# Form stage spread over modes 55 to 61, channel sums moved around mode 62's product, more filler matmuls, and longer store runs

## The chip, the cores and the metric

The kernel runs on one core of a Trainium2 chip. A core has TensorE (PE; its weight loads are shown as PEld), VectorE (DVE), ScalarE (ACT), GpSimd (POOL) and SyncE (SP), a memory of 128 partitions next to the engines (SBUF), an accumulator memory of 8 banks that the matmuls write (PSUM), and 16 DMA engines that move data between SBUF and the main memory. The metric is the time on the device in microseconds, the median of several runs.

## The reference

```python
q_p, k_p = phi(q), phi(k)                 # phi(x) = elu(x) + 1; 8 batches, 8 heads, 576 rows, 64 columns
kv  = einsum('bhsd,bhse->bhde', k_p, v)
z   = sum(k_p, axis=2)
x   = einsum('bhsd,bhde->bhse', q_p, kv) / (einsum('bhsd,bhd->bhs', q_p, z)[..., None] + 1e-6)
x   = x in the shape (8, 576, 512)        # heads side by side
X   = rfft(x, axis=1)[:, :64]             # 64 modes
Y   = einsum('bmd,mde->bme', X, w_r + 1j * w_i)    # one complex 512 x 512 matrix for each mode
u   = x + irfft(Y, n=576, axis=1)
out = u + maximum(u @ w_ch, 0)
```

The two weight tensors w_r and w_i hold 64 matrices of 512x512 in float32 each, 134 MB in all.

## The kernel before

**Attention.** For each batch the kernel loads q, k and v, forms the features, the 64x65 sums over k and v, the attention rows and their Fourier transform (a matmul with a constant matrix). The transformed rows of all batches end up in the tile xt_c.

**Mode pairs.** Then the 64 modes are worked through in 32 pairs (`mode_pair(p)` for modes 2p and 2p+1, `last_pair()` for modes 62 and 63, p = 31). A pair's weights are 2 MB in bfloat16, converted on the way by DMAs that POOL issues (`w_load`, L119; `w_load_last`, L131, cuts the last pair into seven DMAs). From pair 5 on there are two weight buffers: the loads of pair p+2 wait on POOL's queue until the products of pair p (L442) have been done. The products go to a PSUM tile for each mode. VectorE and ScalarE copy them out (`evacuate`, L452, L454), and eight small matmuls (`picks`, L460) bring each mode's rows into a collecting tile, which is copied on after every eighth mode. Inside a pair the order on TensorE is: products, the "mid" slot of other work, picks, the "end" slot, then `keep_warm(FILL[p])`. `keep_warm(n)` issues n matmuls of 128x512 whose result nobody uses (L425, tile zl); they are called fillers below. `pin` keeps the instructions of an engine in the order of the program.

**Other work.** The lists `work` and `slots` spread the work on x between the pairs. `share` hands a list of items out to slots in proportion to weights.
- Pairs 5 to 14: the attention rows again, in the order of the output (36 tiles of 128 rows).
- Pairs 15 to 26, the fold: the inverse transform of modes 0 to 31 is added to x, and x @ w_ch of that is formed and kept as E0 (L653 to L684).
- Pairs 27 to 29, the form stage: for each batch b, `form_z(b)` (eight matmuls, L698, copied out by ScalarE at L703) and `form_y(b)` (eight transposes, L711, copied out by VectorE at L712) make the rows of modes 32 to 55 for the end. After those of batch 0 and of batch 1 come four `fold_lead` items each (L720 to L728). That makes 24 items: "z0, y0, four folds, z1, y1, four folds, z2, y2 ... z7, y7".
- Pair 30: the channel sums of the first two tile pairs. `channels(n)` (L774, two matmuls) brings E0 into an accumulator of two banks, and `first_rows(n)` (L874, two matmuls) adds batch 0's rows of modes 32 to 55. The four PSUM banks of the form stage are given up for these accumulators ahead of pair 30.

**Last pair.** Mode 62's product goes the usual way, with four fillers before its picks and six after them. Mode 63's product (y_last, L504, 32 matmuls with 16 columns) is computed transposed, right after the fillers. Its weights' second half comes in four pieces of 256, 128, 64 and 64 KB.

**Tail.** The rows of modes 56 to 63 are formed (L914 to L925) and sent within SBUF to the other batches' rows (two DMAs, L929). Then the 18 tile pairs follow in turn: `channels(n)`, `rectified(n)` (inverse transform, L735, and Relu, L784) and `finish(n)` (inverse transform, addition to x on VectorE, L816, and the store, L790, on SP's queue). A store of one tile has runs of 2 KB in the output, one of two tiles 4 KB, one of four tiles (the batches in `QUADS`) 8 KB. The last tile pair is added and stored one tile at a time (L811).

Of the kernel before, what the change touches and what calls it, by code (L numbers as in the profile page):

```python
# [14 lines left out]
ALU = mybir.AluOpType  # L15
# [28 lines left out]
def kernel(  # L44
# [10 lines left out]
    nc = tc.nc  # L55
# [12 lines left out]
    NE = NM - NL  # L68
    NF = NM // 2
# [42 lines left out]
    LAST = NM // 2 - 1  # L112
# [309 lines left out]
    def keep_warm(n: int):  # L422

        for _ in range(n):
            pin(nc.tensor.matmul(last_ps[0], id16, wch16[:, 0, :]))  # L425
# [4 lines left out]
    def work_slot(p: int, name: str):  # L430
        for _ in range(slots.get((p, name), 0)):
            if work:
                work.pop(0)()

    def product(P, kk: int, w, dc: int):
        last = kk // 2 == LAST
        n_dc = NDL if last else NDW
        c = dc % NDC * 32
        n = 32 if dc < NDC else 2 * B
        rows = slice(0, 128) if last else HALVES[kk % 2]  # L440
        pin(
            nc.tensor.matmul(  # L442
                P[c : c + n, :], xt_cols(dc, kk, n), w[rows, dc, :],
                start=(dc < NDC), stop=(dc >= n_dc - NDC), tile_position=(rows.start, c),
                skip_group_check=True,
            )
        )

    def evacuate(kk: int, P):
        st = ystage.tile([128, D], F16, tag="ystage", bufs=2, name=f"ys{kk}")  # L450
        if kk % 2 == 0:
            pin(nc.vector.tensor_copy(out=st, in_=P))  # L452
        else:
            pin(nc.scalar.copy(out=st, in_=P))  # L454
        return st
# [9 lines left out]
    def mode_pair(p: int):  # L465
        nonlocal yt_ps
        w = w_get(p)
        kks = (2 * p, 2 * p + 1)
        if p % 4 == 0:
            yt_ps = psW.tile([128, NDC, 8, 2 * B], F32, tag="yt", bufs=1, name=f"yt{p // 4}")  # L470
        Ps = [psW.tile([128, D], F32, tag="P", bufs=2, name=f"P{kk}") for kk in kks]
        for dc in range(NDW):
            for P, kk in zip(Ps, kks):
                product(P, kk, w, dc)
        sts = [evacuate(kk, P) for P, kk in zip(Ps, kks)]
        work_slot(p, "mid")
        for kk, st in zip(kks, sts):
            picks(kk, st)
        if p % 4 == 3:
            if kks[1] < NF:  # L480
                pin(nc.vector.tensor_copy(out=YE_T[:, :, kks[1] - 7 : kks[1] + 1, :], in_=yt_ps))
            else:
                g = (kks[1] - NF) // NL + 1
                pin(nc.vector.tensor_copy(out=YL[:, :, :, g, :], in_=mode_rows(yt_ps)))
        work_slot(p, "end")
        keep_warm(FILL.get(p, 0))

    def last_pair():
        w = w_get(LAST)
        kk = NM - 2  # L490
        P = psW.tile([128, D], F32, tag="P", bufs=2, name=f"P{kk}")
        for dc in range(NDL):
            product(P, kk, w, dc)
        st = evacuate(kk, P)
        keep_warm(4)
        picks(kk, st)
        pin(nc.vector.tensor_copy(out=Y8[:, :, 0 : NL - 1, :], in_=yt_ps[:, :, 0 : NL - 1, :]))
        keep_warm(6)
        kk = NM - 1
        y_last = psW.tile([128, NDC, 2 * B], F32, tag="P", bufs=2, name="y_last")  # L500
        for dc in range(NDL):
            for ec in range(NDC):
                pin(
                    nc.tensor.matmul(  # L504
                        y_last[:, ec, :], w[:, NDL + dc, ec * 128 : ec * 128 + 128],
                        xt_cols(dc, kk, 2 * B),
                        start=(dc == 0 and ec == 0), stop=(dc == NDL - 1), skip_group_check=True,
                    )
                )
        nc.vector.tensor_copy(out=Y8[:, :, NL - 1, :], in_=y_last)  # L510
# [9 lines left out]
    PSUM = bass.MemoryType.PSUM  # L520
    psW = tc.alloc_tile_pool(name="psW", bufs=1, space=PSUM, side="left")
    psB = tc.alloc_tile_pool(name="psB", bufs=1, space=PSUM, side="right")


    n_early = n_keep + n_pre
    FILL = {**{p: 1 for p in range(20, 27)}, 27: 1, 28: 1, 29: 2, 30: 3}
    ystage = ctx.enter_context(tc.tile_pool(name="ystage", bufs=1, side="right"))
    inv_sb = ystage.tile([2 * NM, S], F16, name="inv_sb")
    inv2_sb = ystage.tile([128, S], F16, name="inv2_sb")
# [8 lines left out]
    def mode_rows(ps):  # L538
        return ps.rearrange("p c m (t b) -> p c (m t) b", b=B)
# [19 lines left out]
    def x_of(t: int):  # L559
        if t < B * NJJ:  # L560
            return x_main[t // NJJ][:, t % NJJ, :]
        i = t - B * NJJ
        return x_tail[i // 2][:, i % 2, :]
# [185 lines left out]
    pairs = []  # L749
# [5 lines left out]
    N_PRE = 2  # L755
# [3 lines left out]
    def on_bank(n: int, banks: set, ins):  # L759
        pin(ins)  # L760
        for other, theirs in users.setdefault(n, []):
            if not banks & theirs:
                tc.declare_no_dep(ins.ins, other.ins, reason="the other bank of the pair")
        users[n].append((ins, banks))
    accs: dict[int, object] = {}

    def channels(n: int):
        pool = acc_pools[n % 4 // 2]
        accs[n] = pool.tile([128, 2, D], F32, tag="acc", bufs=2, name=f"acc{n}")
        for i, t in enumerate(pairs[n]):  # L770
            for cols, src in e0_parts(t):
                on_bank(
                    n, {i},
                    nc.tensor.matmul(  # L774
                        accs[n][:, i, cols], id16, src, start=(cols.start == 0), stop=False,
                        skip_group_check=True,
                    ),
                )
# [7 lines left out]
    def store(t: int, n_t: int):  # L786
        if t < B * NJJ:
            b, jj = divmod(t, NJJ)
            r0 = b * S + BASE[b % 2]
            nc.sync.dma_start(  # L790
                out=out_rows[r0 : r0 + 512, :].rearrange("(r j) d -> r j d", j=NJJ)[:, jj : jj + n_t, :],
                in_=x_main[b][:, jj : jj + n_t, :],
            )
            return
        i = t - B * NJJ
        nc.sync.dma_start(
            out=out_rows.rearrange("(i r) d -> r i d", i=B // 2)[512:640, i : i + 2, :],
            in_=x_tail[i // 2],
        )

    QUADS = (6,)

    def finish(n: int):
        acc = accs[n]
        single = n == len(pairs) - 1
        t0 = pairs[n][0]
        add_inverse(n, 0)
        for i, t in enumerate(pairs[n]):
            if single:
                x = x_of(t)  # L810
                on_bank(n, {i}, nc.vector.tensor_tensor(out=x, in0=acc[:, i], in1=x, op=ALU.add))  # L811
                store(t, 1)
        if single:
            return
        x = x_main[t0 // NJJ][:, t0 % NJJ : t0 % NJJ + 2, :] if t0 < B * NJJ else x_tail[(t0 - B * NJJ) // 2]
        on_bank(n, {0, 1}, nc.vector.tensor_tensor(out=x, in0=acc, in1=x, op=ALU.add))  # L816
        if t0 < B * NJJ and t0 // NJJ in QUADS:
            if t0 % NJJ:
                store(t0 - 2, NJJ)
            return  # L820
        store(t0, 2)
# [24 lines left out]
        if b < N_LEAD:  # L846
            work += [lambda t=t: fold_lead(t) for t in range(b * NJJ, b * NJJ + NJJ)]
    n_form = len(work) - n_fold
    first_fold, first_form, n_form_p = NF // 2 - 1, NE // 2 - 1, 3
    fold_pairs = first_form - first_fold  # L850

    def share(n_items: int, steps: list):
# [11 lines left out]
    share(  # L864
        n_form,
        [((first_form, "end"), 6)]
        + [((p, h), 4) for p in range(first_form + 1, first_form + n_form_p) for h in ("mid", "end")],
    )

    def first_rows(n: int):  # L870
        for i, t in enumerate(pairs[n]):
            on_bank(
                n, {i},
                nc.tensor.matmul(  # L874
                    accs[n][:, i], inv2_sb[0 : 2 * NF, rows_of(t, BASE[0])], YZ[0][0 : 2 * NF, 1, :],
                    start=False, stop=False, skip_group_check=True,
                ),
            )
# [8 lines left out]
    )  # L887

    for p in range(n_early, LAST):
        if p == LAST - 1:  # L890
            assert not work
            psB.release()
            acc_pools.append(
                tc.alloc_tile_pool(name="psT0", bufs=1, space=PSUM, side="right", reuse_waits="tile")
            )
            slots[p, "mid"] = slots[p, "end"] = N_PRE
            for n in range(N_PRE):
                work += [lambda n=n: channels(n), lambda n=n: first_rows(n)]
        mode_pair(p)
    last_pair()  # L900


# [14 lines left out]
    for h in range(2):  # L917
        for ec in range(NDC):
# [3 lines left out]
                    start=(ec == 0), stop=(ec == NDC - 1),  # L922
# [5 lines left out]
    for h, eng in enumerate((nc.sync, nc.gpsimd)):  # L928
        eng.dma_start(  # L929
            out=YZ_all[64 * h : 64 * h + 64 : NF // NL].rearrange("r b z d -> r b (z d)"),  # L930
# [11 lines left out]
    def add_one(n: int, i: int):  # L942
# [8 lines left out]
            out=x_of(0), in0=accs[0][:, 0], scalar=0.0, in1=x_of(0), op0=ALU.max, op1=ALU.add  # L951
# [51 lines left out]
```

## Time and profile before

| | |
|---|---|
| median of 4 runs | 425.05 us (423.73 to 425.36) |
| the profiled execution's own time | 423.73 us |
| its span, first to last instruction | 421.9 us |
| busy: PE, DVE, ACT, POOL | 271.9, 215.3, 161.6, 56.6 us |
| mean granted TensorE clock | 0.777 |
| moved by the DMA engines | 93.19 MB, of that 81.47 MB on POOL's queue |
| weight loads, issue to landing | 12.3 us (w_r), 17.0 us (w_i) |
| products L442: idle before them for w_i | 64.3 us |

The page of the profile shows the span in 40 slices of 10.5 us: the busy share of each engine in tenths, the granted TensorE clock (PEclk) in tenths of full speed and the busy share of the DMA engines. The chain of the work that ended last is followed back from the last instruction, at each step to what released it. The view of groups gives busy time and idle time by line; the timeline gives instructions in order, with the idle time before each and what ended it; and the view of stretches gives busy times, clock and DMA share for any stretch of the span. Times in these views are microseconds from the span's start.

### The profile page before, as it was taken

To read this page: it belongs to the slowest core of one execution; us is meant where nothing else is said; L and a number is where in the kernel's file an instruction comes from. 1 tells how busy PE (TensorE), PEld (TensorE's weight loads), DVE (VectorE), ACT (ScalarE), POOL (GpSimd) and SP (SyncE) were. 2 spreads that over 40 slices of the span, in tenths; PEclk is the share of its full clock that TensorE was granted. 3 is DMA by queue.
4 is the path that set the end of the run, shared out by engine and by line. 5 is a ranking of instruction groups with operands and counts; after the bars stand their busy time and mean duration, and the time that the engine had idled before them with its cause. 6 is when DMAs were issued, how large, how long until landed. Compare 5 with 4: busy or idle time off the path is not lost.

```text
span 421.9 us, 7890 instructions
## 1 busy us (share of the span) xinstructions
PE 271.9 (64%) x3378; PEld 148.9 (35%) x3378; DVE 215.3 (51%) x447; ACT 161.6 (38%) x253; POOL 56.6 (13%) x99
## 2 busy tenths in 40 slices
PE   0348378778607644444343677968687795899992
PEld 0246267666402222222122233424243232365420
DVE  3599498886302462464544433445354243322794
ACT  4688577854301102000000243444354251231782
POOL 4222124210001111111111111101011111121000
PEclk9999886889955555555555598789899697679998
DMA  9999999999999999999999999999999999998697
GB/s 214 210 210 215 206 227 194 216 224 217 205 229 209 221 217 211 217 217 214 214 223 214 210 224 214 211 220 219 210 219 217 218 211 219 217 190 162 238 404 305
DMA packets 20802, 93.19 MB, mean 221 GB/s; under 512 B 2080, under 2 KB 11168, under 8 KB 16480
## 3 DMA queue, kind: packets, MB, share of 16 engines
q0 software_dynamic: 16512, 81.47, 94.2%
q1 hardware_dynamic: 4256, 11.22, 7.2%
q8 instruction: 26, 0.43, 0.4%
q14 instruction: 8, 0.07, 0.0%
HBM read 163.93 MB, written 9.44 MB: 411 GB/s over the span
## 4 chain that ended last, share of the span: by engine, by line
DMA 63%; PE 22%; DVE 4%; ACT 4%; issue 3%; POOL 2%; DVEq 0%; POOLq 0%; ACTq 0%
DMA w<-in_moe_w_i_dram 48%; PE P L442 8%; DMA pick_sb<-row_pick 8%; DMA k<-in_k_dram 7%; PE acc L735 3%; PE z L698 2%; PE acc L774 2%; ACT ke L213 2%; POOL w L119 1%; ACT qT L249 1%; PE zl L425 1%; DVE ys L452 1%; PE yp L711 1%; PE yt L460 1%; DVE x L299 1%
## 5 line engine op out<-in xcount | busy, mean ns | idle before, releaser
L442 PE MATMUL P<-w,xt_c 64*32 64x512 bf16 (+2 forms) x1000 | 51.3, 540 | 65.7 <-DMA w<-in_moe_w_i_dram 64.3
L452 DVE CAST ys<-P 128x512 f16<-128x512 f32 x32 | 22.1, 691 | 117.4 <-PE P L442 117.4
L454 ACT CAST ys<-P 128x512 f16<-128x512 f32 x31 | 18.1, 585 | 150.6 <-PE P L442 150.6
L119 POOL DMA_DIRECT2D w<-in_moe_w_r_dram x31 | 16.3, 526 | 245.4 <-PE P L442 114.5
L442 PEld LDWEIGHTS <-xt_c 64*32 64x32 bf16 (+2 forms) x1000 | 17.0, 127 | 83.9 <-DMA w<-in_moe_w_i_dram 47.7
L676 PE MATMUL eps<-wch,xTw 128*128 128x512 f16 x144 | 41.2, 413 | 0.0
L165 PEld LDWEIGHTS <-qT 64*128 64x128 f16 (+1 forms) x640 | 22.9, 123 | 50.5 <-issue 30.9
L165 PE MATMUL num<-kv,qT 64*128 64x65 f16 (+1 forms) x320 | 13.6, 209 | 26.1 <-ACT xt_c L350 12.6
L657 DVE TENSOR_TENSOR x_main<-ya,x_main 128x512 f32<-128x512 f32 x32 | 22.0, 689 | 14.5 <-PE ya L653 14.3
L659 ACT CAST x16w<-x_main 128x512 f16<-128x512 f32 x32 | 19.8, 618 | 23.5 <-DVE x_main L657 22.5
L165 PE MATMUL nw<-kv,qT 64*128 64x65 f16 (+1 forms) x320 | 19.0, 240 | 9.5 <-DVE x_tail L620 4.3
L684 ACT CAST E<-eps 128x512 f16<-128x512 f32 (+1 forms) x40 | 21.2, 540 | 9.7 <-PE eps L676 9.7
L460 PE MATMUL yt<-pick_sb,ys 128*128 128x16 f16 x252 | 11.7, 174 | 17.3 <-DMA pick_sb<-row_pick 10.7
L299 DVE TENSOR_TENSOR x<-num,rd 128x512 f16<-128x512 f32 x32 | 22.1, 691 | 1.1
L242 PE MATMUL qTp<-id,qe 128*128 128x128 f16 x144 | 15.9, 299 | 10.2 <-DVE qe L226 9.7
L213 ACT ACTIVATE qe<-q 128x1152 f16<-128x1152 f16 (+1 forms) x16 | 17.8, 1156 | 11.3 <-DMA q<-in_q_dram 11.3
L249 ACT COPY qT<-qTp 128x1152 f16<-128x1152 f16 x16 | 19.6, 1292 | 0.6 <-PE qTp L242 0.2
L213 ACT ACTIVATE ke<-k 128x1152 f16<-128x1152 f16 x16 | 17.7, 1152 | 4.8 <-DMA k<-in_k_dram 4.8
L460 PEld LDWEIGHTS <-ys 128*128 128x128 f16 x252 | 9.7, 102 | 27.0 <-DVE ys L452 14.9
L784 ACT ACTIVATE acc<-acc 128x512 f32<-128x512 f32 x34 | 18.1, 582 | 2.4 <-PE acc L735 1.6
L242 PEld LDWEIGHTS <-qe 128*128 128x128 f16 x144 | 13.7, 139 | 11.2 <-DVE qe L226 10.1
L119 POOL DMA_DIRECT2D w<-in_moe_w_i_dram x31 | 16.8, 543 | 4.6 <-DMA q<-in_q_dram 2.3
(114 smaller groups left out, 457.6 us busy)
## 6 DMA issues: line engine op xcount, KB each, us to landing
w<-in_moe_w_r_dram POOLq DMA_DIRECT2D x31, 1024.0 KB, 12.3
w<-in_moe_w_i_dram POOLq DMA_DIRECT2D x31, 1024.0 KB, 17.0
out_dram<-x_main SPq DMA_DIRECT2D x11, 512.0 KB, 4.0
k<-in_k_dram POOLq DMA_DIRECT2D x8, 576.0 KB, 12.7
v<-in_v_dram POOLq DMA_DIRECT2D x8, 576.0 KB, 14.8
q<-in_q_dram POOLq DMA_DIRECT2D x7, 576.0 KB, 12.7
out_dram<-x_main SPq DMA_DIRECT2D x6, 256.0 KB, 4.3
q<-in_q_dram SPq DMA_DIRECT2D x2, 576.0 KB, 4.7
```

Source lines behind the costliest of these rows:

```text
L119: nc.gpsimd.dma_start(out=w_in[p][half::2], in_=two.rearrange("g (r dc) e -> (g r) dc e", dc=NDW))
L165: mm = nc.tensor.matmul(num[hpo][orow, c0 : c0 + 65], qT[rows, hpp, h2, cols], kv_sb[rows, hpp, h2, :])
L213: pin(nc.scalar.activation(out=ev[:, c], in_=heads(nm, b, c), func=AF.Exp))
L242: nc.tensor.transpose(qT_ps[:, j], phi["q", b][:, c, j].rearrange("p o d -> p (o d)"), id16,)
L249: nc.scalar.copy(out=qT[:, :, c * NJ : (c + 1) * NJ], in_=qT_ps.rearrange("p j x -> p x j"))
L299: nc.vector.tensor_tensor(out=dst.rearrange("p (o c d) -> p o c d", o=2, c=4), in0=nv[:, :, :, 0:64], in1=rden.unsqueeze(3).broadcast_to([ ...
L442: nc.tensor.matmul(P[c : c + n, :], xt_cols(dc, kk, n), w[rows, dc, :], start=(dc < NDC), stop=(dc >= n_dc - NDC), tile_position=(rows.sta ...
L452: pin(nc.vector.tensor_copy(out=st, in_=P))
L460: nc.tensor.matmul(yt_ps[:, ec, kk % 8, :], st[:, ec * 128 : ec * 128 + 128], pick_sb)
L657: pin(nc.vector.tensor_tensor(out=x, in0=acc, in1=x, op=ALU.add))
L676: nc.tensor.matmul(e_ps, xT[:, c, :], wch16[:, c, :], start=(c == 0), stop=(c == NDC - 1))
L684: pin(nc.scalar.copy(out=dst, in_=e_ps[:, cols]))
```

## The change

It has five parts.
1. The form stage's 24 items are handed out up to the "end" slot of pair 30 (mode 61), not 29. `n_form_p` goes.
2. The form stage's PSUM banks are given up after pair 30, and the two channel sums move from pair 30 into `last_pair()`: the first ahead of mode 62's product (a new slot "start"), the second between its copy and its picks, where four fillers stood. Three fillers instead of six follow.
3. `FILL` is 5 for pairs 18 to 26 (before: none for 18 and 19, 1 for the others), 8 for 27 (1), 2 for 28 (1), 7 for 29 (2) and 7 for 30 (3).
4. `QUADS` holds batches 2, 4, 5 and 6 instead of 6 alone.
5. The last tile pair is added and stored like the others, in one piece.

```diff
     def last_pair():
         w = w_get(LAST)
         kk = NM - 2
+        work_slot(LAST, "start")
         P = psW.tile([128, D], F32, tag="P", bufs=2, name=f"P{kk}")
         for dc in range(NDL):
             product(P, kk, w, dc)
         st = evacuate(kk, P)
-        keep_warm(4)
+        work_slot(LAST, "mid")
         picks(kk, st)
         pin(nc.vector.tensor_copy(out=Y8[:, :, 0 : NL - 1, :], in_=yt_ps[:, :, 0 : NL - 1, :]))
-        keep_warm(6)
+        keep_warm(3)
...
-    FILL = {**{p: 1 for p in range(20, 27)}, 27: 1, 28: 1, 29: 2, 30: 3}
+    FILL = {**{p: 5 for p in range(18, 27)}, 27: 8, 28: 2, 29: 7, 30: 7}
...
-    QUADS = (6,)
+    QUADS = (2, 4, 5, 6)

     def finish(n: int):
         acc = accs[n]
-        single = n == len(pairs) - 1
         t0 = pairs[n][0]
         add_inverse(n, 0)
-        for i, t in enumerate(pairs[n]):
-            if single:
-                x = x_of(t)
-                on_bank(n, {i}, nc.vector.tensor_tensor(out=x, in0=acc[:, i], in1=x, op=ALU.add))
-                store(t, 1)
-        if single:
-            return
...
     share(
         n_form,
         [((first_form, "end"), 6)]
-        + [((p, h), 4) for p in range(first_form + 1, first_form + n_form_p) for h in ("mid", "end")],
+        + [((p, h), 4) for p in range(first_form + 1, LAST - 1) for h in ("mid", "end")]
+        + [((LAST - 1, "mid"), 2), ((LAST - 1, "end"), 1)],
     )
...
     for p in range(n_early, LAST):
-        if p == LAST - 1:
-            assert not work
-            psB.release()
-            acc_pools.append(
-                tc.alloc_tile_pool(name="psT0", bufs=1, space=PSUM, side="right", reuse_waits="tile")
-            )
-            slots[p, "mid"] = slots[p, "end"] = N_PRE
-            for n in range(N_PRE):
-                work += [lambda n=n: channels(n), lambda n=n: first_rows(n)]
         mode_pair(p)
+    assert not work
+    psB.release()
+    acc_pools.append(
+        tc.alloc_tile_pool(name="psT0", bufs=1, space=PSUM, side="right", reuse_waits="tile")
+    )
+    slots[LAST, "start"] = slots[LAST, "mid"] = N_PRE
+    for n in range(N_PRE):
+        work += [lambda n=n: channels(n), lambda n=n: first_rows(n)]
     last_pair()
```

More of the change, by code (lines that the diff above doesn't have):

```diff
@@ L848 @@
     n_form = len(work) - n_fold
-    first_fold, first_form, n_form_p = NF // 2 - 1, NE // 2 - 1, 3
+    first_fold, first_form = NF // 2 - 1, NE // 2 - 1
     fold_pairs = first_form - first_fold
```

## The prediction

> **What bounds the kernel now.** First the slices of the page: over the whole weight stream the DMA row stands at 9, and from slice 12 on the clock row falls to 5 and recovers only in part.
>
> ```profile
> PEclk9999886889955555555555598789899697679998
> DMA  9999999999999999999999999999999999998697
> ```
>
> So the weights (2 MB a pair, every 9.7 us) set the time up to the last pair, as long as the matmuls free each weight buffer in time. Second, the chain that ended last, to find where this stops being so. Columns: start, length, what.
>
> ```profile
> 342.41 17.39 DMA w<-in_moe_w_i_dram
> ...
> 359.85 1.95 PE P L442 x24
> 361.79 1.92 PE z L698 x8
> ...
> 371.53 0.44 PE yp L711 x7
> 371.96 1.72 PE z L698 x7
> 373.69 0.54 PE zl L425
> 374.22 1.03 PE P L442 x29
> ...
> 388.07 1.31 PE zl L425 x6
> 389.38 0.92 PE y_last L504 x32
> ```
>
> Up to 359.8 it hops from one weight load to the next; from pair 28 (modes 56, 57) on it is TensorE work without a gap: pair 29's product starts at 374.2. Its weights had been issued at 352.07 with 17.4 us to landing, so they lay there from 369.5: TensorE was 4.7 us late. Third, what this costs. The last pair's loads (L131) need pair 29's buffer, so they go out only then; and the DMA runs dry (columns: stretch, length, busy of PE, PEld, DVE, ACT, POOL, clock, DMA share, GB/s).
>
> ```profile
> 375.62 0.52 POOL L131 DMA_DIRECT2D w<-in_moe_w_r_dram  x1 [12.40 <-PE P L442]
> ```
> ```profile
> 370.00:375.00 5.00, 5.00 (x57) 2.35 (x53) 0.42 (x1) 1.41 (x3) 0.00 (x0) 0.59 1.05 223
> 375.00:376.00 1.00, 1.00 (x28) 0.81 (x14) 0.68 (x2) 0.58 (x1) 0.38 (x1) 1.00 0.47 98
> 376.00:378.00 2.00, 2.00 (x24) 1.66 (x20) 0.77 (x3) 0.59 (x1) 1.75 (x4) 1.00 0.80 156
> ```
>
> Lost: 0.53 x 1.0 + 0.20 x 2.0 = 0.9 us; since packets count where they start, I take 0.7 to 0.9. The last 64 KB piece, issued at 380.44 and 9.3 us under way, lands at 389.8; the last product y_last runs 389.2 to 390.3 because the ten fillers ahead of it end at 389.2. Fourth, the stores at the end:
>
> ```profile
> 398.00:402.00 4.00, 4.00 (x29) 1.20 (x28) 3.97 (x4) 3.39 (x7) 0.00 (x0) 1.00 0.98 389
> 406.00:412.00 6.00, 6.00 (x35) 1.54 (x35) 6.00 (x6) 5.36 (x11) 0.00 (x0) 1.00 1.03 409
> 416.00:419.00 3.00, 0.00 (x0) 0.00 (x0) 0.00 (x0) 0.00 (x0) 0.00 (x0) 0.91 1.00 382
> ```
>
> From 394 to 419 the DMA is full and the last compute ends at 415.8: the tail is the 9.4 MB of stores, and it shifts as a block with y_last.
>
> **What the skill says.** "TensorE: Matmul & The Clock Gate", Part 1 (The HAM clock gate), says the array runs at half clock after an idle window of about 3.4 us and at full clock after a busy one. The trace agrees: the stretch 278.52 to 281.93 has 0.47 us of TensorE work, the next 3.41 us are granted 0.50, and after that (busy) stretch the clock is 1.00 again. The page's section "HAM oscillation — how this bites in real kernels" describes short products between DMA waits that lose the clock each time; here 350.19 to 353.61 was busy for 1.83 of 3.42 us and the next 10 us ran at 0.50. "DMA: Bandwidth & Descriptors", "Issuing engines are not separate DMA queues", says all queues share the same 16 engines: so one late weight load can't be made up elsewhere, and stores are paid in total bytes and run lengths, as the tail windows show.
>
> **The change part by part.** The sum is against the profiled execution: span 421.9, time 423.73 (1.8 around it). The median of the four runs is 425.05, 1.3 above it; the trace doesn't show why, so I carry the difference over unchanged.
>
> *Fillers, modes 36 to 53.* Five for pairs 18 and 19, four more for 20 to 26: 38 matmuls of 128x512. Six of them took 1.31 us (chain above), 0.22 each; at half clock about 0.43 (one L676 group of four took 1.91 against 1.03). Up to 1.1 us a pair (2.2 cold), ahead of a wait: the products waited for weights 64.3 us in 22 waits. Where the wait is shorter (0.63 us before the product at 340.43) the product is late by the rest; the release of its buffer has about 4 us to spare, because pair 29's 4.7 us cost less than 1 us of DMA. So 0 on the end; without that cover 1.1 us a pair, 10 us in all. They may save re-warming in the fold stage, which is hidden too.
>
> *Form stage.* There are 24 items in this order: z0, y0, four folds of batch 0, z1, y1, four folds of batch 1, then z and y of batches 2 to 7. The old weights (6,4,4,4,4 of 22) give 6,4,5,4,5; the new ones (6,4,4,4,4,2,1 of 25) give 5,4,4,4,4,2,1. They issue no DMA. Pair 28 loses y2 and z3 (0.44 + 1.86 to the next step), gains one matmul of batch 0 (0.4) and one filler (0.2 to 0.5): 14.3 - 2.3 + 0.7 = 12.7 us with the old clock. At full clock: product 1.04, two z 1.86 (0.93 each in the chain after 375), y 0.52 and its copy 0.6, four folds about 3.0 (DVE's 0.69 add sets their pace), one matmul 0.22, picks 0.29, fillers 0.43: 8.0. Pair 27's eight fillers take 1.7 to 3.4 us after about 357.2, reach 358.9 to 360.6, and so fill most of the wait in which the clock was lost; at worst they make pair 28 0.7 late. I take the full clock from about 361 on: pair 28 ends near 368, pair 29's product starts at 369.5, and the L131 loads go out near 371, with pair 30's still running to 379.2 (362.67 + 16.5). The DMA gap of 0.7 to 0.9 goes; the last piece lands at about 389.0.
>
> *Is TensorE there by then?* Pair 29: product 1.04, y2 z3 y3 z4 2.9, picks 0.3, y4 z5 y5 z6 2.9, seven fillers 1.6: 8.7, ends 378.3, before pair 30's landing. Pair 30 from 379.25: product 1.04, y6 z7 1.4, picks 0.3, y7 0.5, fillers 1.6: 384.1. The moved channel sums of the first two tile pairs (four matmuls each: 0.53 + 0.55 in the chain) now stand on TensorE's queue, the first ahead of mode 62's product, the second behind it in place of four fillers: 1.08 to 385.2; product 0.59 (landed before, 384.06 less the gap): 385.8; second sum 1.08, picks 0.2, three fillers 0.65: 387.7. Behind them waits y_last, for weights landing to 389.0; its last four matmuls need about 0.3: end 389.3 against 390.3. So TensorE has 0.7 us to spare at the end (after the first 28 matmuls), 0.9 at pair 30 and 1.4 at pair 29. Gain 0.9 to 1.0; I take 0.9.
>
> *Stores.* 18 stores from x_main become 14, four with 8 KB runs. The one such store before ran at 416 GB/s (413 to 415), 4 KB at 409, the 2 KB runs at 383 (417 to 419): 3.1 MB gain 0.13 us, the last 512 KB at 4 KB instead of 2 KB 0.09. Against that, a first half waits for its second, 1.17 us (400.05 to 401.22 in batch 2). Up to 400 the queue holds some 0.8 us of work after the store before it (1.9 of the 2.2 MB issued are moved), so the engines may idle for up to 0.4; later the backlog covers the hold. I take 0.2: tail 0, between -0.3 and +0.4. The last add becomes one of 1.22 in place of two of 0.68 and ends at 415.8 as before; its store goes out while two others are queued.
>
> Sum: -0.9 + 0: span 421.0, time 422.8 on the profiled basis, 424.2 on the median.
>
> **The rivals.** *The gain is larger:* the unprofiled runs, 1.2 to 1.6 slower, lose more clock in modes 56 to 61, and that goes as well: 424.2 - 1.3 = 422.9. For it: the free phase of the 3.4 us window; against: the profiled run already had pair 28 mostly at half clock, so 1.5 us is about all that is left. *No gain:* the fillers don't hold the clock. Then pair 28 takes 12.7 us from 359.85 or 360.4 to at most 373.1, L131 goes out 0.5 to 1 us earlier, and the added work eats that: pair 29 8.7 (8.0 before) to 381.8, from pair 30's start to y_last 8.45 (7.0 before) to 390.2, y_last 1.1: it ends at 390.7 to 391.3 against 390.3: 425.5 to 426.0. For it: clock 0.50 from 367.26 to 374.09, in the middle of this work. *Slower, TensorE becomes the bound:* the same, and half clock also through a part of pairs 29 and 30. There is no slack left then, and each window of 3.41 us at half clock adds 1.7 us: one puts the kernel at 427.4, and it decides from the first one on. Against it: a late TensorE has no waits, and the gapless work from 367 was at full clock by 374. *Stores run dry* at each held half: +0.5 in place of -0.2, with the gain: within 0.3%; without it 425.7.
>
> **Numbers.** The likeliest, 424.2 (own range 423.5 to 424.9), 0.48; larger gain 0.18; no gain 0.19; slower 0.10; stores 0.05. A difference of 0.3% (1.3 us: below 423.8, above 426.3) is about what a measurement can tell from none. Faster: 0.18 and the lower edge of the first, 0.26; slower: 0.10 and the upper edges of "no gain" and "stores", 0.16; between them 0.58. The range 422.7 to 426.3 leaves out the slower case and the edges of the others.
>
> **What would show it.** Right: the L131 wait ends near 371; no stretch between 370 and 387 with a DMA share below 0.95; clock 1.00 from about 361; y_last ends 0.3 after its last landing; last add near 415. Wrong: a clock of 0.5 after 365, pair 30's product later than 380, a filler group directly ahead of y_last with no wait between, or DMA share below 0.9 where batch 2's first half is held.

## The result, and the profile after

The changed kernel takes 425.88 us (median of 43 runs, 424.57 to 426.52) against 425.14 us for the kernel before (64 runs, 423.48 to 425.80): a ratio of 1.0021, 95% interval 1.0014 to 1.0029. It is slower by 0.2%, some 0.9 us; the forecast was 0.9 us faster. The profiled execution of after took 425.88 us with a span of 424.0 us, that of before 423.73 and 421.9. The executions of before fall into two groups (23 of the 64 at 423.48 to 424.26, median 423.74; 41 at 424.48 to 425.80, median 425.33), and its first profile came from the lower group, so the two profiles differ by more (2.1 us) than the medians. After has two groups as well (15 runs at 424.57 to 425.30, 28 at 425.60 to 426.52), each about 1 us above its counterpart: medians 424.97 and 426.09.

The slices of the page of after come first. A slice is 10.6 us. Behind the long run of 5s the clock row has one 6 left, from 350 to 360 us, and then 8, 8 (before 7, 6, 7 there). In the DMA row the hollow between the weights and the stores, 382 to 403, reads 5, 7 (before 8, 6).

```profile
PEclk9999686889955555555555598989899996889997
DMA  8999999999999999999999999999999999995797
```

The chain that ended last, of after (start, length, what):

```profile
369.27 1.92 PE z L699 x8
371.19 0.97 PE zl L425 x2
372.16 1.87 PE P L442 x19
...
380.09 1.62 PE zl L425 x7
381.71 1.03 PE P L442 x29
...
385.20 1.62 PE zl L425 x7
...
387.80 0.59 PE P L442 x8
...
389.67 0.66 PE zl L425 x3
390.33 0.92 PE y_last L505 x32
```

Pair 29's product (372.16) still runs on a half clock: 1.87 us for what takes 1.03 at 381.71. From 369 on TensorE has no gap, and the three fillers at 389.67 stand directly ahead of y_last (390.17 to 391.24 by its first and last matmul; before 389.22 to 390.29). That is one of the signs that the prediction had named as wrong.

The timeline of after shows the last pair's first load, 1.2 us earlier than before:

```profile
374.39 0.52 POOL L131 DMA_DIRECT2D w<-in_moe_w_r_dram  x1 [10.94 <-PE P L442]
```

And the windows of after (stretch, length, busy time of PE, PEld, DVE, ACT, POOL, clock, DMA share, GB/s):

```profile
370.00:375.00 5.00, 5.00 (x54) 1.87 (x52) 0.91 (x2) 1.17 (x2) 0.61 (x2) 0.59 0.99 210
375.00:376.00 1.00, 1.00 (x16) 0.96 (x14) 0.12 (x1) 0.38 (x1) 1.00 (x3) 1.00 1.12 188
376.00:378.00 2.00, 2.00 (x28) 1.61 (x28) 0.56 (x2) 0.80 (x2) 0.52 (x1) 1.00 0.98 205
386.00:389.00 3.00, 3.00 (x19) 0.97 (x18) 0.56 (x1) 0.00 (x0) 0.00 (x0) 1.00 0.57 102
402.00:403.00 1.00, 1.00 (x10) 0.32 (x8) 0.97 (x2) 0.87 (x2) 0.00 (x0) 1.00 0.03 8
421.30:422.50 1.20, 0.00 (x0) 0.00 (x0) 0.00 (x0) 0.00 (x0) 0.00 (x0) 0.50 0.07 27
```

Four things are to be seen. The DMA gap at 375 to 378 is closed (shares 0.47 and 0.80 before, 1.12 and 0.98 now), and nothing came of it. The weights don't end together: in 386 to 389 the share is 0.57 on average. A new gap of one microsecond stands in the stores, at 402 (share 0.03; before 1.04). And at the very end, 421.3 to 422.5, the share is 0.07, about one engine in sixteen: the others have ended by 421.3, and one works on alone to 422.59.

What that last line comes from isn't in the diff. The page of the profile also lists the DMA queues, two of them with the kind "instruction". Queue 8 is one of these; in after it reads (packets, MB, share of 16 engines; in before it had 26 packets):

```profile
q8 instruction: 27, 0.44, 0.4%
```

Its packets have 16 KB, and their number follows that of TensorE's instructions (matmuls and weight loads together): 6756 in before with 26 packets, 6852 in after with 27, that is one for 254 to 260. So they are taken here for the fetches of TensorE's program; e8 below, with 256 instructions more than before, bears this out. Most of them occupy a DMA engine for 0.9 to 1.0 us (median 0.95 in after, single ones in the runs up to 1.7). The 48 fillers that the change adds net are 96 instructions and shift the fetches. By the packet records the last ones start at 373.7, 385.2 and 397.8 in before, and at 380.7, 390.6 and 415.1 in after. The last falls into the full store tail, as the queues of after in 413 to 417 show:

```profile
q1 hardware_dynamic: 215, 1.59, 97.8%
q8 instruction: 1, 0.02, 1.4%
```

### The profile page after: what moved, and what is told of

Same layout as the page of the kernel before. It is cut to its first block, busy times and chain, and to the rows that moved or that the text cites. A ratio compares the mean times of both kernels' runs of the same rounds, so it can differ in the third digit from the quotient of the medians.

```text
span 424.0 us, 7976 instructions
## 1 busy us (share of the span) xinstructions
PE 279.7 (66%) x3426; PEld 152.7 (36%) x3426; DVE 215.3 (51%) x446; ACT 161.5 (38%) x253; POOL 56.5 (13%) x99
## 4 chain that ended last, share of the span: by engine, by line
DMA 63%; PE 22%; DVE 4%; ACT 4%; POOL 2%; issue 2%; DVEq 0%; POOLq 0%; ACTq 0%
DMA w<-in_moe_w_i_dram 48%; DMA pick_sb<-row_pick 8%; PE P L442 7%; DMA k<-in_k_dram 7%; PE acc L736 3%; PE z L699 2%; PE acc L775 2%; PE zl L425 2%; ACT ke L213 2%; POOL w L119 1%; ACT qT L249 1%; PE yp L712 1%; DVE ys L452 1%; PE yt L460 1%; PE yb L721 1%
## 5 line engine op out<-in xcount | busy, mean ns | idle before, releaser
L442 PE MATMUL P<-w,xt_c 64*32 64x512 bf16 (+2 forms) x1000 | 49.6, 525 | 59.5 <-DMA w<-in_moe_w_i_dram 58.1
L677 PE MATMUL eps<-wch,xTw 128*128 128x512 f16 x144 | 40.0, 405 | 0.0
L425 PE MATMUL zl<-wch,id 128*128 128x512 f16 x72 | 19.6, 408 | 0.0
```

Of the source, the lines that this page charges most:

```text
L442: nc.tensor.matmul(P[c : c + n, :], xt_cols(dc, kk, n), w[rows, dc, :], start=(dc < NDC), stop=(dc >= n_dc - NDC), tile_position=(rows.sta ...
L677: nc.tensor.matmul(e_ps, xT[:, c, :], wch16[:, c, :], start=(c == 0), stop=(c == NDC - 1))
```

## The experiments

The parts are numbered as above: 1 form stage, 2 channel sums, 3 fillers, 4 and 5 stores. Letters in the expectations are short for theories, roughly these: T, the held first halves leave the DMA idle in the tail; P, TensorE's queue (fillers and moved sums) makes y_last late; F, the fetch of instructions falls into the store tail; L, the DMA engines that lag behind set the end of the weights; W, the clock lost after the wait ahead of y_last makes the two groups of times. "Tail" below is the time from the issue of the first store to the end of the span. Ratios are to executions of the kernel before that were measured alongside; with two groups of times in each they need not equal the quotients of the medians.

### Which part

**e1**, the stores alone on the kernel before:

```diff
-    QUADS = (6,)
+    QUADS = (2, 4, 5, 6)
...
-        single = n == len(pairs) - 1
...
-        for i, t in enumerate(pairs[n]):
-            if single:
...
```

> The kernel before with parts 4 and 5 alone (8 KB runs for batches 2, 4, 5, 6; the last tile pair in one piece). Theory T (the store queue runs dry): in the profile of the changed kernel no packet moves from about 402.1 to 403.0, because the first half of batch 2 is held back and a store moves its first packet only some 0.9 us after its issue; this loses about 1 us, the longer runs give back 0.3: slower by 0.4 to 1.0 us, with one stretch of about 0.9 us without DMA work some 8 us after the first store. The prediction's reading (hold 0.2, runs -0.2): 0, between -0.3 and +0.4, and no such stretch.

Measured: 423.65 us, ratio 0.9983 [0.9970, 0.9997]; profiled 423.87, span 422.1. Windows of e1 (columns as above):

```profile
401.00:403.00 2.00, 2.00 (x16) 0.57 (x12) 1.92 (x3) 1.61 (x5) 0.00 (x0) 1.00 0.59 242
420.00:421.00 1.00, 0.00 (x0) 0.00 (x0) 0.00 (x0) 0.00 (x0) 0.00 (x0) 0.50 0.45 176
```

The hole that the held half makes is there (0.41 x 2.0 = 0.8 us of DMA time), and still the kernel isn't slower: the tail is 28.0 us against 28.25, and all engines end together (the others at 420.64, the last at 420.75). So the theory that the stores by themselves make the kernel slower (T) is wrong in its sign. Why a hole of 0.8 us costs nothing was not settled; that the hold lets late engines catch up and the longer runs give the rest back is only argued.

**e2**, after with the old stores (parts 1 to 3):

```diff
-    QUADS = (2, 4, 5, 6)
+    QUADS = (6,)
...
+        single = n == len(pairs) - 1
...
```

> The changed kernel with the old stores (parts 1 to 3 alone). Theory P (TensorE's queue sets the end of y_last): the added fillers stand between pair 29 and y_last, which starts when they end, near 390.2, and ends near 391.2: slower than before by 0.3 to 0.9 us in the median, and the stretch without DMA work near 402 is gone. If the stores were the whole loss: 0 within 0.2. The prediction's main case (gap closed, weights 0.7 to 0.9 us earlier): faster by 0.7 to 0.9.

Measured: 425.34, ratio 1.0023 [1.0013, 1.0033]. Without the new stores the loss is there all the same. So it sits in parts 1 to 3.

**e3**, after without the hold in batch 2:

```diff
-    QUADS = (2, 4, 5, 6)
+    QUADS = (4, 5, 6)
```

> The changed kernel with 8 KB runs for batches 4, 5 and 6, batch 2 in two stores as before. Theory T: the queue is not yet deep at batch 2 and is deep later, so only batch 2's hold costs: 0.7 to 1.0 us faster than the changed kernel, and no stretch without DMA work in the tail. If every hold costs or none does: within 0.3 of the changed kernel.

Measured: 425.26, ratio 1.0008 [0.9998, 1.0018]. It lies between; its interval touches that of after. In its trace the stretch 402 to 403 is full (share 1.01), so the hold of batch 2 may be worth some 0.5 us here, but this run doesn't prove it.

**e4**, parts 1 and 2 alone, that is e2 with the old filler table:

```diff
-    FILL = {**{p: 5 for p in range(18, 27)}, 27: 8, 28: 2, 29: 7, 30: 7}
+    FILL = {**{p: 1 for p in range(20, 27)}, 27: 1, 28: 1, 29: 2, 30: 3}
```

> Parts 1 and 2 alone: the form stage spread to mode 61 and the channel sums moved, but the fillers of the tables as before (three before y_last) and the old stores. The DMA share should stay near 1.0 between 375 and 378, as in the changed kernel. Prediction's main case: the last weight piece lands 0.7 to 0.9 us earlier than before, y_last ends 0.7 to 1.0 earlier, the kernel is 0.6 to 1.0 us faster. Theory L (laggards): about half of the DMA engines run 2 to 3 us behind the others and never stood idle in that gap, so the last landing stays where it was (389.5 to 390.5) and the kernel is within 0.4 us of before.

Measured: 424.5, ratio 0.9993 [0.9979, 1.0006]. Between e2 and e4 lie the fillers alone. By its interval e4 can't be told from before, and y_last ends at 390.33 there, no earlier than in before, where the prediction's main case had it 0.7 to 1.0 us earlier. In e2 it ends at 391.42: this looked like TensorE's queue (P). But the tails say something else: 28.9 in e2 and 29.1 in e3, 28.5 in e4 and 28.0 in e1. The long ones are those with an instruction packet at 414 to 415 (e2 414.3, e3 414.5; after 415.1, tail 29.4). The next runs separate the two.

### Late fillers or instruction fetch

**e5**, the kernel before with 48 fillers more, all in modes 16 to 39, far from the end:

```diff
-    FILL = {**{p: 1 for p in range(20, 27)}, 27: 1, 28: 1, 29: 2, 30: 3}
+    FILL = {**{p: 4 for p in range(8, 20)}, **{p: 1 for p in range(20, 28)}, 28: 1, 29: 2, 30: 3}
```

> The kernel before with 48 more fillers, all in pairs 8 to 19, where TensorE waits some 4 us a pair for weights: TensorE then has as many instructions (6852) as in the changed kernel, and nothing else is changed. Theory F (fetch of TensorE's instructions): every 256 instructions one 16 KB packet of the instruction queue takes one DMA engine for about 0.95 us; the added instructions move the last fetches from about 385 and 398 to about 380, 390 and 414 to 415, and in the tail one DMA engine then ends its stores 1.0 to 1.5 us after the others (0.3 before): slower by 0.4 to 1.0 us in the median. Theory P (only the place of the fillers at TensorE counts): 0 within 0.2.

**e6**, after with its late fillers (modes 54 to 61), but modes 36 to 53 as before:

```diff
-    FILL = {**{p: 5 for p in range(18, 27)}, 27: 8, 28: 2, 29: 7, 30: 7}
+    FILL = {**{p: 1 for p in range(20, 27)}, 27: 8, 28: 2, 29: 7, 30: 7}
```

> The changed kernel with pairs 18 to 26 filled as before (38 fillers fewer, 6776 TensorE instructions, 20 more than before); the fillers of pairs 27 to 30 as in the change. Theory F: no fetch at 414, one near 396 to 398; no lone engine at the end; faster than the changed kernel by 0.5 to 1.0 us. Theory P: y_last still starts when the fillers end, near 390; as slow as the changed kernel within 0.3. Both at work: between, 0.3 to 0.6 faster than the changed kernel.

**e7**, the whole change with the old filler table:

```diff
-    FILL = {**{p: 5 for p in range(18, 27)}, 27: 8, 28: 2, 29: 7, 30: 7}
+    FILL = {**{p: 1 for p in range(20, 27)}, 27: 1, 28: 1, 29: 2, 30: 3}
```

> The whole change without its added fillers (the table as before; 6742 TensorE instructions): form stage to mode 61, channel sums moved, new stores. Theories P and F both say that the loss goes: y_last ends with the last landing, near 390.3, no fetch at 414, the stores as in the run with the stores alone: 0.3 to 1.0 us faster than the kernel before, at least 1 us faster than the changed kernel.

**e8**, after with 80 fillers more in modes 12 to 35. With their weight loads these are 160 instructions, so that the total is 256 above that of before and the fetches come back to where before had them:

```diff
-    FILL = {**{p: 5 for p in range(18, 27)}, 27: 8, 28: 2, 29: 7, 30: 7}
+    FILL = {**{p: 7 for p in range(6, 14)}, **{p: 6 for p in range(14, 18)}, **{p: 5 for p in range(18, 27)}, 27: 8, 28: 2, 29: 7, 30: 7}
```

> The changed kernel with 80 more fillers in pairs 6 to 17, where TensorE waits: 7012 TensorE instructions, 256 more than the kernel before, so that the fetches fall where they fall there. Theory F: fetches near 385 and 398 instead of 380, 390 and 414, no lone engine at the end of the stores, 0.5 to 1.0 us faster than the changed kernel. Theory P alone: within 0.2 of the changed kernel (or slower, by what the fillers themselves cost).

Measured:

| kernel | us | ratio | last fetches at | tail, us | y_last ends |
|---|---|---|---|---|---|
| e5 | 425.48 | 1.0010 [1.0000, 1.0020] | 391.2, 414.8 | 28.97 | 391.66 |
| e6 | 424.64 | 0.9984 [0.9971, 0.9996] | 382.7, 395.1 | 28.0 | 390.06 |
| e7 | 424.13 | 0.9987 [0.9977, 0.9998] | 385.1, 398.0 | 28.05 | 390.08 |
| e8 | 423.67 | 0.9982 [0.9973, 0.9991] | 383.6, 397.8 | 28.14 | 390.79 |
| before, after | | 1, 1.0021 | 397.8; 415.1 | 28.25; 29.4 | 390.29; 391.24 |

e8 decides between F and P. It is after with more work for TensorE, and it takes 0.9982/1.0021 = 0.996 of after's time, 1.7 us less, more than the 0.5 to 1.0 expected; the two intervals lie far apart. The profiles give the same 1.7 (spans 424.0 and 422.3): some 1.3 in the tail, 0.4 in an earlier first store. Here are its windows at the end (columns as above), with no lone engine:

```profile
419.00:421.00 2.00, 0.00 (x0) 0.00 (x0) 0.00 (x0) 0.00 (x0) 0.00 (x0) 0.50 0.81 315
421.00:422.50 1.50, 0.00 (x0) 0.00 (x0) 0.00 (x0) 0.00 (x0) 0.00 (x0) 0.50 0.00 0
```

And its queues from 405 to 421.9, in which no queue 8 appears:

```profile
q1 hardware_dynamic: 1571, 6.32, 93.1%
q14 instruction: 1, 0.01, 0.1%
```

Its last fetch, at 397.8 as in before, falls among the stores too, but more than 20 us before their end, and it leaves no lone engine. The stores still pause after it (DMA share 0.64 in 402 to 403); that the engine catches up in such pauses is only argued.

e5 is the counterpart: nothing but 48 fillers, the last of them more than 100 us before the end, a loss of 0.4 us whose interval reaches down to nothing, and again a fetch at 414.8 and one engine that ends its stores late (the others at 421.17, it at 422.32). Of the 2.1 us by which its profile is longer than that of before, only the 0.7 in the tail goes with the fetch: the first store is 1.4 us late (395.03), after a half clock that lasts from 354.7 to 375.2, as it is in e10 below without such a fetch. The trace doesn't name the DMA engine of a packet; that the late one is the one with the instruction packet is inferred: after, e2, e3 and e5, and no others, have a fetch at 414 to 415 together with one engine that works on alone for a microsecond or more, and the delay has about the length of one packet.

e6 goes against P as it was put: with after's late fillers, all of them, y_last (388.56 to 390.06) waits for its weights and not for fillers. What differs is the clock. In e6 it is 1.00 from 361 on; in after it is 0.50 from 367 to 374. e2, e3, e8 and e9, whose y_last is late as well, keep it in 370 to 375, wait for pair 30's weights soon after (1.5 to 1.8 us of TensorE work in the 3.4 us before 382, in e6 2.6) and lose it then. In e8:

```profile
378.20:381.61 3.41, 1.75 (x43) 1.04 (x44) 0.46 (x1) 0.37 (x1) 0.00 (x0) 1.00 1.01 209
381.61:385.03 3.42, 3.42 (x28) 1.76 (x27) 0.99 (x3) 0.80 (x2) 0.00 (x0) 0.50 1.01 208
```

e6 is also the prediction's main case come true on TensorE: the clock holds, the last loads go out at 371 as forecast, and no DMA engine stands still in 374 to 380. Its timeline and chain:

```profile
370.97 0.52 POOL L131 DMA_DIRECT2D w<-in_moe_w_r_dram  x1 [7.97 <-PE P L442]
```

```profile
375.79 13.94 DMA w<-in_moe_w_i_dram
...
389.77 0.30 PE y_last L505 x4
```

The loads go out 4.65 us earlier than in before and have landed at 389.7, as in before (389.8): closing the gap gained nothing. e7 says the same from the other side. Its windows:

```profile
375.00:376.00 1.00, 1.00 (x14) 0.93 (x14) 0.69 (x2) 0.34 (x1) 1.00 (x2) 1.00 0.47 98
376.00:378.00 2.00, 2.00 (x32) 1.62 (x28) 0.42 (x1) 1.06 (x2) 1.09 (x3) 1.00 1.03 184
```

A part of the gap is there again (by the packet records 0.3 us on the mean of the engines, 0.7 in before), and yet the kernel is a little faster than before, while after has no gap and is slower. The packet records tell why (L): in eleven of the fourteen profiles the engines other than the slowest end the weights at 388.5 to 388.8 (in e5, e8 and e10 at 389.1 to 389.5), with the gap (before 388.75, e7 388.75) or without it (after 388.67, e6 388.57). In after about half of the 16 engines end at 386.2 to 386.8 (the share falls step by step from 386 on) and half at 388.6 to 388.7. In the gap of before at least 9 of the 16 engines were always at work. That those which stood still were the ones that were ahead anyway is inferred, since the trace doesn't name them, but e5 supports it: its gap is twice as long (1.5 us on the mean), and there nearly all engines are at work up to 389.

```profile
376.00:378.00 2.00, 2.00 (x40) 1.51 (x26) 1.02 (x2) 0.59 (x1) 1.00 (x2) 1.00 0.58 123
386.00:389.00 3.00, 3.00 (x21) 0.84 (x17) 0.56 (x1) 0.00 (x0) 0.00 (x0) 1.00 0.96 175
```

After the others one engine goes on alone (in e8 two), to 389.5 in before, 390.2 in after and 391.0 in e5; it sets the very last landing. Why it takes longer in some profiles than in others is not shown.

### Counter-checks, and the two groups

**e9**, after with 14 fillers fewer, so that the last fetch falls before the stores:

```diff
-    FILL = {**{p: 5 for p in range(18, 27)}, 27: 8, 28: 2, 29: 7, 30: 7}
+    FILL = {**{p: 4 for p in range(20, 24)}, **{p: 5 for p in range(24, 27)}, 27: 8, 28: 2, 29: 7, 30: 7}
```

> The changed kernel with 14 fillers fewer (none in pairs 18 and 19, four instead of five in 20 to 23), 6824 TensorE instructions instead of 6852. Theory F: the last-but-one fetch moves 28 instructions later, from 390.6 to about 392 or 393, into the stretch in which no weights and no stores move, and the last one, which came at 415 as TensorE ended, is not reached; no lone engine at the end: 1.0 to 1.7 us faster than the changed kernel. Theory P alone: within 0.2 of the changed kernel.

Measured: 424.45, ratio 0.9991 [0.9976, 1.0006]; last fetch at 391.6, tail 28.1. Against after (1.0021 from 1.0014 up) that is a gain of 0.3%, 1.3 us. Since y_last is late here too (391.38), it is the tail that gained. The hole in the stores is here as well (share 0.12 in 402 to 403), so it isn't the hole that made after's tail long. And 14 fillers fewer help about as much as 80 more: it isn't their number.

**e10**, e5 with 34 fillers in place of 48:

```diff
-    FILL = {**{p: 1 for p in range(20, 27)}, 27: 1, 28: 1, 29: 2, 30: 3}
+    FILL = {**{p: 3 for p in range(8, 18)}, **{p: 2 for p in range(18, 20)}, **{p: 1 for p in range(20, 28)}, 28: 1, 29: 2, 30: 3}
```

> The kernel before with 34 more fillers in pairs 8 to 19 (6824 TensorE instructions), beside the run with 48. Theory F: last fetch at about 392 to 393, none at 414: no slower than the kernel before (-0.5 to +0.2), where 48 fillers cost 0.4. If the number of fillers costs by itself: +0.3.

Measured: 424.76, ratio 0.9995 [0.9983, 1.0007]; last fetch at 392.0, tail 28.25 against 28.97 in e5. The direction is right, but the intervals of e5 and e10 overlap a little; by itself this pair would not be enough.

**e11**, the kernel before, unchanged, profiled once more (an empty diff).

> The kernel before, profiled once more, to see what differs between an execution near 423.7 (the one profiled first) and one near 425.2, if it is one. The larger-gain rival of the prediction: the later L131 and more half clock in modes 56 to 61, y_last ends 1 to 1.5 us later. Otherwise: a lone DMA engine at the end of the weights or of the stores, or half clock between y_last and the first store.

Measured: 425.46 us, span 423.7: this profile is of the upper group. Its timeline, windows and chain:

```profile
372.65 0.52 POOL L131 DMA_DIRECT2D w<-in_moe_w_r_dram  x1 [9.65 <-PE P L442]
```

```profile
388.20:391.60 3.40, 2.40 (x44) 2.07 (x45) 0.52 (x2) 0.51 (x2) 0.00 (x0) 1.00 0.06 10
391.60:395.00 3.40, 3.37 (x11) 1.16 (x9) 1.38 (x2) 2.07 (x5) 0.57 (x1) 0.50 0.38 102
```

```profile
388.83 1.11 PE y_last L504 x28
...
392.45 1.86 PE acc L735 x4
```

The last loads went out 3 us earlier than in the first profile (372.65, not 375.62), since the half clock that stood there from 367 to 374 is missing here, and y_last ends at 390.27 as there (390.29). By the packet records no engine stands still in 374 to 380: this is the closed gap on the unchanged kernel, once more worth nothing. But now TensorE waits ahead of y_last (nothing from 388.2 to 388.8), the stretch 388.2 to 391.6 is busy for 2.40 of 3.40 us, and the next 3.4 us are granted half the clock. The first inverse product of the tail takes 1.86 us (1.02 in after), and the stores run dry for a while; the tail is 29.7 us. In the first profile the same stretch was busy for 3.08 us and kept its clock:

```profile
388.20:391.60 3.40, 3.08 (x49) 2.30 (x48) 1.05 (x3) 0.49 (x2) 0.00 (x0) 1.00 0.09 14
391.60:395.00 3.40, 3.15 (x16) 1.51 (x14) 2.32 (x4) 2.61 (x7) 0.57 (x1) 1.00 0.41 112
```

So an earlier weight stream can even cost: the time gained is spent waiting, and the clock goes. e4 is a second sighting: there TensorE waits 1.08 us ahead of y_last, works for 1.96 of the 3.41 us before 390.93, has half the clock in the 3.41 us after, and issues its first store at 394.72, 1.1 us later than before, though y_last ends at the same time. Busy time alone doesn't tell which stretch loses the clock: in after 363.83 to 367.24 is busy for 2.89 us and the next stretch has 0.50, in e12 377.00 to 380.42 is busy for 2.46 and the next has 1.00. What does tell is open.

**e12**, e6 with four fillers more in that wait:

```diff
-        keep_warm(3)
+        keep_warm(7)
```

> The changed kernel with pairs 18 to 26 filled as before, as in the earlier run of that kind, and seven instead of three fillers ahead of y_last (four more, 0.9 us; in that run's profile TensorE waits 0.78 us there). Theory W (a wait ahead of y_last leaves a 3.4 us window too empty, and the chain from y_last to the first stores then runs at half clock, which costs some 1.4 us in a part of the executions, as in the second profile of the kernel before): the executions near 424.7 become rare, median 423.2 to 423.8, faster than the kernel before by 1 us or more. If the two groups of times have another cause: the median stays near 424.6, or gets worse by up to 0.3 where y_last starts later.

Measured: 423.90, ratio 0.9986 [0.9976, 0.9996]. Of e6's 14 runs eight lie at 424.58 to 424.92; of e12's 22 runs two lie above 424.5. Of the 27 executions of before measured alongside e12, 16 lie above 424.5, so the groups are there for the kernel before. The upper group of e6 nearly goes when the wait is filled. The median, 423.9, is a little above the 423.2 to 423.8 that was expected and hardly a gain on the better kernels (0.6 us against before by the ratio, where 1 or more was expected), as the lower group rose from about 423.4 to 423.8.

## Why the prediction was wrong

The forecast was 0.9 us faster, the measurement is some 0.9 us slower; 425.88 us lies inside 422.7 to 426.3, but on the other side of before. The term that carried the forecast was never there, and a term that was put at nothing cost time. Step by step:

- **"The DMA gap of 0.7 to 0.9 goes; the last piece lands at about 389.0."** This is the step that failed. The gap went (L131 at 374.39, shares 0.99 to 1.12), but the last weights landed at 390.45, not at 389.0 (before 389.79). The step took a mean over 16 engines for time lost on all of them. Those that stood still in the gap were, as far as the packet records show, the ones that end some 2 us early; the others set the end, and with or without the gap they end at 388.5 to 388.8 (e6, e7, e11). e6 has all that the step asks for, with the loads at 370.97, and its weights land at 389.7. The gain of 0.9 was never there. The further 0.7 us by which after's last landing is later is that of its one slowest engine, and its cause is open.
- **"Fillers, modes 36 to 53 … So 0 on the end."** The named cover held: the waits swallow their run time (the products wait 58.1 us for weights in place of 64.3). What was missing from the sum is that instructions are DMA traffic. The 96 TensorE instructions moved a 16 KB fetch into the end of the tail, and the tail grew from 28.25 to 29.4 us. With the fetches moved back, the same change is at 0.9982 (e8). The Trainium skill, "DMA: Bandwidth & Descriptors", section "Issuing engines are not separate DMA queues", was quoted for all queues sharing the same 16 engines. The runs agree with it for the instruction queue too (one engine late by about one packet); that queue was listed on the page of before and left out of the sum.
- **"I take the full clock from about 361 on."** Wrong in the profiled execution: 0.59 in 370 to 375. It came true in e6, and up to 381 or 382 in e2, e3, e8 and e9. Pair 29's product started at 372.16 in place of 369.5. From there the sums were close: 9.55 us to pair 30's product (8.7 forecast at full clock), then 8.46 us from there to y_last (8.45 forecast in the rival). The rival "no gain" had y_last end at 390.7 to 391.3 and the time at 425.5 to 426.0; measured 391.24 and 425.88. Its picture of TensorE fits the profile. That its time fits as well is luck in part, for it has no fetch in it. As the cause of the loss it isn't enough: e9 has y_last as late and is not slower than before. The rival "slower", one more window at half clock and 427.4, didn't come about: the windows of after in 375 to 378 and 386 to 389 show 1.00.
- **"Stores … I take 0.2: tail 0."** About right as to the stores alone: e1's tail is 0.25 us shorter than that of before. Two terms were off. The engines stood still for about 1 us in after and 0.8 in e1, not "up to 0.4": in after the next store is issued at 402.16 and its first packets move at 403.0; and this hole cost less than its length.
- **"1.3 above it; the trace doesn't show why."** e11 shows one cause, in one profile: a half clock from 391.6 on, after a wait ahead of y_last. The rival "the gain is larger" had looked for the difference in modes 56 to 61; there e11 is earlier than the first profile, not later. The Trainium skill's section "HAM oscillation — how this bites in real kernels" ("TensorE: Matmul & The Clock Gate") has the clock lost in DMA waits of 3 to 5 us between short products. Here the trace has the loss after a wait of only 0.7 us, in a stretch that was busy for 2.40 of 3.40 us; where they differ, the measurement decides.

The balance of the profiles: the first store 0.95 us later (394.60 against 393.65) and the tail 1.15 longer make the 2.1 us between the spans. The medians differ by less. Most runs of before (41 of 64) are in the group that lies 1.6 us higher, and e11 and e12 put that group down to the clock after the wait. How the runs of after divide these losses is not shown run by run: only one was profiled.

The best version measured is e8: 423.67 us, ratio 0.9982 [0.9973, 0.9991], faster than both kernels by more than its interval. e1, e6, e7 and e12, with 0.9983 to 0.9987, can't be told from it.

## What to carry to other kernels

Before you count idle DMA time as lost, find out whether the engines that end last were idle in it; a mean share of 0.5 can cost nothing. An instruction that is hidden on its own engine is still fetched by a DMA engine: look where the instruction queue's packets fall, and keep them away from the end of a full stretch in which every engine must end together. And profile more than one execution when the times fall into groups: the one that you see need not be the typical one.

## What the runs showed of the hardware

- An instruction packet of 16 KB occupied one DMA engine for 0.9 to 1.0 us in most cases, about once in 256 TensorE instructions (26 packets for 6756, 27 for 6852). One of them near the end of a full tail lengthened it by 0.7 us (e5 against e10) to 1.3 us (after against e8 and e9); one at 397.8, early in the stores, left no lone engine (before, e8).
- The 16 engines drift apart in a long stream of weights: in after about half of them end some 2 us behind the rest, though all have had work from 374 to 386.
- A single stretch of 3.4 us, 71% busy and with a wait of 0.7 us, was followed by half the clock for the next 3.4 us (e11), and that execution took 1.7 us more than the one of the same kernel that kept its clock; filling the wait with four matmuls made the upper group rare (2 of 22 in e12, 8 of 14 in e6).
